# Weight conversions ahead of the first FFN: fourteen pieces in steps 1 to 94 instead of thirteen in steps 1 to 113

## The chip, the core and the metric

The kernel runs on one core of a Trainium2 chip. The metric is the device time of one execution in microseconds; the median of three executions stands for the kernel before. TensorE, VectorE (DVE), ScalarE (ACT), GpSimd (POOL) and SyncE (SP, which here only issues transfers) each work through an order of their own and wait for each other by semaphores. That order is fixed when the kernel is built.

## What is computed

The inputs are q, k and v of 8 batches, 12 heads, 448 tokens and 64 values a head, in float32, and two weight matrices of 768 x 3072 and 3072 x 768, stored as 64-bit floats.

```python
q_n, k_n = rmsnorm(q, g_q), rmsnorm(k, g_k)
attn = softmax(scale * q_n @ k_n.T) @ v        # per batch and head
x = attn                                       # as (batch, 448, 768)
u = x + real(fft(fft(x, axis=1), axis=2))
un = (u - mean(u)) / sqrt(var(u) + 1e-6)       # over the 768
out = u + maximum(un @ w_ch1, 0) @ w_ch2
```

## The kernel before

**Stages.** Each batch goes through attention, then the spectral part (the two Fourier transforms as matmuls, then the tiles `u` and `un`), then the FFN. `aux(b)` is a generator that yields after each small step of attention and spectral part of batch b; `ffn(b, unT)` is one that yields after each piece of weights. Attention works on six pairs of heads, each with softmax rows (`softmax_pair`), the norm and transposes of the next pair (`transpose_pair`) and the product with v (`value_pair`). `fold` prepares the Fourier transform along the 768 on VectorE. At the start, all 114 steps of `aux(0)` (0 to 113) run without an FFN beside them. Steps 0 to 94 are attention up to the point at which `attention(0)` fills the list `mixing`; in steps 95 to 113, which hold the last product with v, the last fold and the spectral part, each step is followed by one of the first fourteen steps of `aux(1)`. After that `merge` runs `ffn(0)` with the rest of `aux(1)`, `ffn(1)` with `aux(2)`, and so on.

**Weights.** The weights come as doubles. A piece is either 128 columns of w_ch1 (24 pieces, 128x768 values) or a 512x128 block of w_ch2 (36 pieces, 128x512 values): sixty in all. `convert` (from line 765) brings one piece in and splits it into a high and a low part for TensorE. It issues a DMA of the raw words into a tile `dbl` (L773, two buffers, tag X); ScalarE makes a float of the high words into a tile `mag` (L776, two buffers) and scales the low words in place (L777); VectorE clamps (L778), shifts (L782) and merges (L786); POOL adds the low part (L790); ScalarE rounds to the high part (L791); VectorE subtracts for the low part (L792). The result lies in one of three buffers of its stream and is also stored to DRAM (L820), from where later batches load it ready-made (L832).

**Two streams and early pieces.** Pieces are used in the order of the list `PIECES`; two streams of three buffers each hold them, in batch 0 by even and odd place. A stream's `load` takes its next piece: in batch 0 it converts it, unless the piece is in the set `early`; such a piece, and every piece of later batches, is loaded ready-made. The set is filled by `convert_some`, which is called after each step of `aux(0)` but the first, and which asks for a piece as soon as its account passes 1:

```python
conv = (p for n, p in enumerate(PIECES) if n % 8 in (3, 6))
def convert_some(share):
    debt[0] += share
    while debt[0] >= 1:
        p = next(conv)
        streams[stream_of(0, p)].converted(p, "e" + ...)
        early.add(p)
        debt[0] -= 1
```

In the trace the tiles of early pieces are named `dble`, `mage`, `w1e` and `w2e`; those of the pieces that the streams convert are `dbl`, `mag` and `w`. With 0.12 a step, pieces 1 to 13 are asked for after steps 9, 17, 25, 34, 42, 50, 59, 67, 75, 84, 92, 100 and 109. The twelfth and fourteenth in the list are 512x128 blocks of w_ch2, the thirteenth is a column piece of w_ch1. Once the 114 steps are through, each stream is asked for three pieces (`streams[n % 2].load()`, six in all), and then for another each time a piece has been used.

**What sets the order.** A scheduler of the framework orders each engine's instructions, in general by their place in the program, and lets a later instruction go first where an earlier one is not ready by its own estimate. The arithmetic of early pieces has one more rule: while `starting[0]` holds, `behind` puts each such instruction after the one that stands fourth from last among those already given to its engine by the other work. An early piece can therefore run only little ahead of the step after which it was asked for. Its DMA has no such rule. The main loop around the change (from line 1094):

```python
for n, _ in enumerate(aux(0)):
    if n == DFT_STEP:
        load_dft()
    if mixing:
        for _ in range(1):
            if next(ahead, None) is not None:
                next(second)
    if n:
        convert_some(CONVERT_EARLY)
starting[0] = False
```

Where all engines' operations go through one helper, the trace gives its line: L115 is the recorder of VectorE, ScalarE and POOL calls, so such instructions are told apart by their tiles. Other lines here: L644 is the first spectral matmul, L689 the write of `u` to DRAM, L888 the transposes of `un`, L1019 and L1040 the FFN's matmuls.

Of the kernel before, what the change touches and what calls it, by code (L numbers as in the profile page):

```python
# [38 lines left out]

RATIO = 0.49  # L40
RATIO_FIRST = 0.6
CONVERT_EARLY = 0.12
EARLY = 2
DFT_STEP = 40
AHEAD = 14
# [46 lines left out]
def spectral_block(ctx, tc, q, k, v, g_q, g_k, w1, w2, d1, d2, out, nb=B):  # L92
# [111 lines left out]
    def load_dft():  # L204
        nc.sync.dma_start(D1.rearrange("r i a n -> r (i a n)"), d1)
        st = slot("PT", "d2s")[:N1, : 4 * N1].rearrange("s (n t) -> s n t", n=4)
        for r in rows_of(N1):
            nc.sync.dma_start(st[r], d2[r].rearrange("s (n t) -> s n t", n=4))
        d2v = D2.rearrange("s i c a t -> s (i c) a t")
        A.copy(d2v[:, :, 0], st)  # L210
        sub(d2v[:, :, 1], st, d2v[:, :, 0])
# [321 lines left out]
    mixing = []  # L533
# [218 lines left out]
    def aux(b):  # L752

        EO, uns[b] = [], {}
        yield from attention(b, EO)
        yield from spectral(b, xTs[b], EO, uns[b])
# [117 lines left out]
# [5 lines that stand above are left out]
            streams[stream_of(0, p)].converted(p, "e" + "_".join(str(x) for x in p))  # L879
            early.add(p)  # L880
            debt[0] -= 1
# [215 lines left out]
# [4 lines that stand above are left out]
            for _ in range(1):  # L1101
                if next(ahead, None) is not None:
                    next(second)
        if n:
            convert_some(CONVERT_EARLY)
    starting[0] = False
    for n in range(6):
# [31 lines left out]
```

## Time and profile before

| what | value |
|---|---|
| median of three executions | 2156.36 us (2156.23 to 2157.32) |
| the profiled execution, its own time | 2157.21 us |
| its span in the trace | 2155.4 us |
| mean granted TensorE clock | 0.984 of full speed |
| DMA over the span | 423.88 MB, 197 GB/s |

The profile is that of one execution. Busy time of an engine is the time in which it ran an instruction of the program; TensorE's matmuls are pipelined and their ends are modelled, so a busy TensorE need not be one at its peak. The share of PEld (weight loads) says more of that. In the windows of the next section each row gives the stretch and its length, then for each engine the busy time and the number of instructions, the granted TensorE clock, the DMA engines' busy share, and GB/s. The chain of waits is followed back from the last instruction, at each step to what released it or to the instruction before it on its engine; its rows are start, length, and what it was.

### The profile page before, as it was taken

How to read it: one execution, taken by the hardware profiler on the slowest of the kernel's cores; microseconds unless marked ns; L12 is line 12 of the kernel's file. 1: busy time of each engine (PE TensorE's matmuls, PEld its weight loads, DVE VectorE, ACT ScalarE, POOL GpSimd, SP SyncE). 2: the span in 40 equal slices, each digit the busy share in tenths (PEclk: the TensorE clock that was granted, in tenths of full speed). 3: DMA queues.
4: the chain of work that ended last, by engine and by line, in shares of the span. 5: the costliest groups of instructions: out<-in, count | busy, mean ns of one | idle time of the engine just before them, and what ended most of it. 6: DMA issues, size and time to landing. Idle time of an engine off the chain costs nothing.

```text
span 2155.4 us, 31372 instructions
## 1 busy us (share of the span) xinstructions
PE 2079.3 (96%) x11256; PEld 1848.5 (86%) x11256; DVE 1544.9 (72%) x3002; ACT 1028.5 (48%) x2218; POOL 343.9 (16%) x200
## 2 busy tenths in 40 slices
PE   7877999999999999999999999999999999999998
PEld 4546777889999999999999999999999989999998
DVE  6787778887885788868787688857787578754122
ACT  6757876455552555335552455425553355422100
POOL 4324333321110111101110111101110011000000
PEclk8987999999999999999999999999999999999999
DMA  6547886687556855667566765558556674458874
GB/s 179 155 124 265 263 256 217 229 276 209 174 164 187 245 168 159 188 203 217 165 177 177 222 197 174 171 183 245 170 164 188 200 210 138 146 177 248 235 246 153
DMA packets 292913, 423.88 MB, mean 197 GB/s; under 512 B 181348, under 2 KB 219221, under 8 KB 292757
## 3 DMA queue, kind: packets, MB, share of 16 engines
q1 hardware_dynamic: 288322, 419.75, 64.1%
q10 hardware_dynamic: 4434, 2.11, 0.4%
q8 instruction: 90, 1.47, 0.3%
q14 instruction: 67, 0.54, 0.1%
HBM read 362.01 MB, written 65.31 MB: 198 GB/s over the span
## 4 chain that ended last, share of the span: by engine, by line
PE 79%; DVE 7%; DMA 6%; ACT 3%; issue 2%; POOL 2%; SPq 1%; POOLq 0%; DVEq 0%; ACTq 0%
PE o L1040 29%; PE h L1019 28%; PE S L407 5%; PE av L519 4%; PE pt L507 4%; DMA dbl<-w 3%; PE y L644 2%; POOL mag L790 1%; PE qk L343 1%; DVE mn L115 1%; DVE mag L786 1%; PE oT L976 1%; DMA u_dram<-u 1%; PE un L888 1%; DVE mag L778 1%
## 5 line engine op out<-in xcount | busy, mean ns | idle before, releaser
L1040 PE MATMUL o<-hs,w 128*128 128x448 f32 x3456 | 792.2, 372 | 4.9 <-DVE acc L115 3.2
L1019 PE MATMUL h<-unT,w 128*128 128x448 f32 x3456 | 783.0, 371 | 4.3 <-DVE hs L115 1.5
L1040 PEld LDWEIGHTS o<-hs,w 128*128 128x128 f32 x3456 | 637.7, 188 | 62.1 <-DVE acc L115 4.2
L1019 PEld LDWEIGHTS h<-unT,w 128*128 128x128 f32 x3456 | 640.0, 189 | 57.8 <-issue 2.2
L115 ACT ACTIVATE P<-S,mn 112x448 f32<-112x448 f32 x384 | 244.0, 638 | 222.5 <-DVE mn L115 208.7
L115 DVE TENSOR_REDUCE mn<-S 112x1 f32<-112x448 f32 x384 | 234.1, 617 | 43.3 <-PE S L407 34.1
L115 ACT ACTIVATE hs<-h 128x448 fp32r<-128x448 f32 x192 | 104.3, 543 | 277.9 <-PE h L1019 277.1
L115 DVE SCALAR_TENSOR_TENSOR hs<-h,hs 128x448 fp32r<-128x448 f32 x192 | 119.1, 620 | 129.8 <-ACT hs L115 128.4
L115 DVE TENSOR_TENSOR acc<-o,acc 128x448 f32<-128x448 f32 (+1 forms) x240 | 146.6, 613 | 87.9 <-PE o L1040 86.9
L115 POOL TENSOR_TENSOR qkn<-raw 112x1024 f32<-112x1024 f32 x36 | 69.4, 1927 | 686.4 <-PE qk L343 409.4
L115 POOL TENSOR_TENSOR ss<-ss,nhalf 112x16 f32<-112x16 f32 x48 | 142.0, 2959 | 203.8 <-DVE ss L115 195.1
L115 ACT CAST T<-pt 128x448 fp32r<-128x448 f32 x216 | 113.6, 533 | 124.7 <-PE pt L507 122.8
L115 DVE TENSOR_TENSOR T<-pt,T 128x448 fp32r<-128x448 f32 x216 | 132.3, 618 | 35.2 <-ACT T L115 34.1
L519 PE MATMUL av<-T,vhl 128*128 128x448 f32 x432 | 152.1, 384 | 0.0
L115 DVE TENSOR_SCALAR P<-P,sm 112x448 f32<-112x448 f32 x288 | 129.2, 487 | 4.6
L407 PE MATMUL S<-KD,QT 128*112 128x448 f32 x328 | 128.6, 392 | 2.2 <-ACT KD L115 1.9
L507 PE MATMUL pt<-ident,P 112*128 112x112 f32 x864 | 126.5, 258 | 0.0
L407 PE MATMUL S<-rounded,QT 128*112 128x448 f32 x328 | 120.4, 367 | 0.2 <-DVE rounded L115 0.2
L507 PEld LDWEIGHTS pt<-ident,P 112*128 112x128 f32 x864 | 104.3, 140 | 16.6
L790 POOL TENSOR_TENSOR mag<-mag,dbl 128x512 uint32<-128x512 uint32 (+1 forms) x47 | 78.8, 1677 | 159.3 <-DVE mag L786 131.2
L115 POOL TENSOR_TENSOR rstd<-st,nhalf 112x1 f32<-112x1 f32 (+2 forms) x32 | 19.6, 612 | 487.5 <-DVE st L115 480.5
L519 PEld LDWEIGHTS av<-T,vhl 128*128 128x128 f32 x432 | 80.9, 188 | 7.9
(120 smaller groups left out, 2499.5 us busy)
## 6 DMA issues: line engine op xcount, KB each, us to landing
w<-w SPq DMA_DIRECT2D x192, 768.0 KB, 4.5
w<-w SPq DMA_DIRECT2D x288, 512.0 KB, 3.9
dbl<-w SPq DMA_DIRECT2D x29, 512.0 KB, 4.8
dbl<-w SPq DMA_DIRECT2D x18, 768.0 KB, 4.9
raw<-q SPq DMA_DIRECT2D x96, 112.0 KB, 2.9
raw<-k SPq DMA_DIRECT2D x96, 112.0 KB, 5.0
values<-v SPq DMA_DIRECT2D x96, 96.0 KB, 4.4
u_dram<-u SPq DMA_DIRECT2D x24, 336.0 KB
```

Source lines behind the costliest of these rows:

```text
L115: ins = emit(*args, **kwargs)
L343: nc.tensor.transpose(pt[:, c * C : (c + 1) * C], qk[:, i, c].rearrange("t h d -> t (h d)"), ident[:C, :C],)
L407: ins = nc.tensor.matmul(s_, QT[:, h, cs], K[:, h], start=step == 0, stop=step == 1)
L507: nc.tensor.transpose(pt[:, c * C : (c + 1) * C], Pc[c][:, 512 * h + j * 128 : 512 * h + (j + 1) * 128], ident[:C, :C],)
L519: nc.tensor.matmul(av[:, :S], lv, T[:, i], start=(j == 0 and i == 0), stop=False)
L644: nc.tensor.matmul(o, src[:, par, t0 : t0 + n], D1[:, ri, par, cols], start=i != 1, stop=i != 0,)
L778: behind(nc.vector.tensor_scalar(out=value, in0=value, scalar1=MIN_HIGH, scalar2=MAX_HIGH, op0=ALU.max, op1=ALU.min,))
L786: behind(nc.vector.scalar_tensor_tensor(out=bits, in0=high, scalar=0xC0000000, in1=bits, op0=ALU.bitwise_and, op1=ALU.bitwise_or,))
L790: behind(nc.gpsimd.tensor_tensor(out=bits, in0=bits, in1=low, op=ALU.add))
L888: nc.tensor.transpose(pt[:, OFFS[i] : OFFS[i] + LENS[i]], uns[i][:, p * 128 : (p + 1) * 128], ident[: LENS[i], : LENS[i]],)
L1019: pace(nc.tensor.matmul(o, w[:, a, c], unT[c][:, z], start=n == 0, stop=n == 17))
L1040: pace(nc.tensor.matmul(o, w[:, a, f], hs[4 * g + f][:, z], start=n == 0, stop=n == 11))
```

## The change

The rate goes from 0.12 to 0.15 a step, and a step asks for conversions only while the list `mixing` is empty, which is so after steps 1 to 94. Pieces 1 to 14 are then asked for after steps 7, 14, 20, 27, 34, 40, 47, 54, 60, 67, 74, 80, 87 and 94. The fourteenth, a block of w_ch2 that has place 54 of 0 to 59 in the order of use, is no longer converted in the FFN of batch 0.

```diff
-CONVERT_EARLY = 0.12
+CONVERT_EARLY = 0.15
...
-        if n:
+        if n and not mixing:
             convert_some(CONVERT_EARLY)
```

## Rows read from the trace of the kernel before

**Rows 1.** The page, busy time of each engine, its share and instructions

```profile
PE 2079.3 (96%) x11256; PEld 1848.5 (86%) x11256; DVE 1544.9 (72%) x3002; ACT 1028.5 (48%) x2218; POOL 343.9 (16%) x200
```

**Rows 2.** Windows by stage: PE, PEld, DVE, ACT, POOL busy, clock, DMA share, GB/s

```profile
0.00:126.00 126.00, 98.58 (x457) 59.13 (x457) 94.52 (x159) 86.21 (x198) 46.27 (x35) 0.89 0.58 171
126.00:158.00 32.00, 23.15 (x126) 16.39 (x124) 25.67 (x48) 17.06 (x39) 6.64 (x3) 0.84 0.32 99
158.00:182.00 24.00, 8.33 (x40) 6.80 (x40) 20.44 (x45) 16.14 (x25) 10.52 (x7) 0.64 0.67 219
182.00:472.00 290.00, 274.32 (x1390) 231.88 (x1391) 234.93 (x407) 192.55 (x375) 102.79 (x64) 0.98 0.77 251
```

**Rows 3.** Windows, tile mage (early pieces): DVE, ACT, POOL busy; sum from 20 us

```profile
126.00:158.00 32.00, 2.20 (x4) 1.27 (x2) 1.44 (x1) 0.84 0.32 99
158.00:182.00 24.00, 3.35 (x4) 1.75 (x2) 1.83 (x1) 0.64 0.67 219
sum 162.00, DVE 34.88 ACT 19.70 POOL 20.89; mean DVE 4.98 ACT 2.81 POOL 2.98
```

**Rows 4.** Windows, tile mag (pieces converted by the streams): DVE, ACT, POOL busy

```profile
158.00:182.00 24.00, 10.04 (x11) 4.39 (x5) 6.03 (x3) 0.64 0.67 219
182.00:472.00 290.00, 119.00 (x177) 63.84 (x89) 72.81 (x44) 0.98 0.77 251
```

**Rows 5.** Chain of waits, 20 to 126 us: first and last of 31 conversion pieces

```profile
28.22 0.07 ACT w2e L791
...
122.84 0.84 ACT w2e L791
```

**Rows 6.** Chain of waits, 126 to 158 us: first and last of three conversion pieces

```profile
138.83 0.33 DVE mage L782
...
145.03 0.60 DVE w1e L792
```

**Rows 7.** Chain of waits, 157 to 183 us

```profile
160.29 0.47 DVE mage L778
...
161.63 0.54 DVE mag L778
...
163.64 2.01 DVE mag L782
...
170.21 0.74 ACT w L791
...
170.97 0.97 DVE w L792
171.94 0.92 ACT mag L776
...
172.89 0.56 DVE mag L778
...
173.95 6.57 DMA u_dram<-u
```

**Rows 8.** Timeline of the DMA queue on SP: start, length, issue

```profile
122.83 0.37 SPq L773 DMA_DIRECT2D dble<-w  x1
...
143.73 0.38 SPq L773 DMA_DIRECT2D dbl<-w  x1
```

**Rows 9.** Timeline, ScalarE: start, length, instruction

```profile
148.23 0.93 ACT L777 ACTIVATE dbl<-dbl 128x768 uint32<-128x768 uint32 x1 [3.88 <-DMA dbl<-w]
...
159.69 0.90 ACT L776 ACTIVATE mag<-dbl 128x768 f32<-128x768 f32 x1
```

**Rows 10.** Timeline, VectorE and POOL, 161 to 166 us

```profile
161.16 0.55 DVE L782 TENSOR_SCALAR mage<-mage 128x768 uint32<-128x768 uint32 x1
...
163.40 1.83 POOL L790 TENSOR_TENSOR mage<-mage,dble 128x768 uint32<-128x768 uint32 x1 [19.69 <-ACT un L115]
...
163.57 2.08 DVE L782 TENSOR_SCALAR mag<-mag 128x768 uint32<-128x768 uint32 x1
```

**Rows 11.** Windows, one full stretch of a later batch, columns as in rows 2

```profile
500.00:510.00 10.00, 10.00 (x60) 9.08 (x59) 9.03 (x20) 7.46 (x18) 1.89 (x1) 1.00 0.85 257
```

## The prediction

> **What bounds the kernel now.** I read the page first, then the stages by windows, then the conversions by their tiles in the same windows, then the chain of waits inside each stage.
>
> The page says that TensorE is busy for 96% of the span [rows 1]; the question is where the other 4% lies. The windows by stage answer it [rows 2]. I cut the span at 126 us (the last step before the mixing of the two batches is through; eleven early pieces are converted), at 158 us (the spectral part of batch 0 begins its last leg), at 182 us (the first FFN matmul) and at 472 us (FFN of batch 0 ends). I call the stages A, B, C, D, and E the rest. In A, B and C TensorE is busy 98.6 of 126, 23.2 of 32 and 8.3 of 24 us; in D 274.3 of 290. Beyond 472 us a typical stretch has TensorE busy 10.00 of 10 us with its weight loads at 9.08 [rows 11], so E has nothing to give. What the change can move lies in the first 472 us.
>
> In A, VectorE is busy 94.5 of 126 us (75%), in B 25.7 of 32 (80%), in C 20.4 of 24 (85%) [rows 2]. So up to 182 us the end is set by a chain that runs through VectorE and ScalarE, and conversions compete there. In D conversions share VectorE too, but TensorE is nearly full.
>
> The conversions are uneven. The early ones cost VectorE 34.88 us for thirteen, 2.68 us each; stage B holds only one (four VectorE instructions, 2.20 us) and C one (3.35 us) [rows 3]. C also holds eleven VectorE instructions, 10.04 us, of the pieces that the streams convert when the early ones are done: at four a piece 2.7 pieces, the other 44.3 being in D with 119.00 us [rows 4]. Of C's 20.4 us of VectorE, 13.4 are conversion.
>
> Why B is so empty shows in two places. Early piece 13 was asked for by the DMA queue at 122.83 us, and the next conversion load left only at 143.73 [rows 8]; there are two buffers for raw doubles, and the thirteenth piece sat in one of them until its arithmetic ran in C. The first stream piece had its low words scaled by ScalarE at 148.23 us, but its other ScalarE step came at 159.69 [rows 9], behind the thirteenth piece's. So the thirteenth, asked for at step 109, holds up all that follow it.
>
> **The change, part by part.** It does two things. The rate goes from 0.12 to 0.15 a step, and steps with mixing under way (95 to 113) ask for nothing. 113 steps by 0.12 made thirteen pieces, eleven of them by step 94; 94 by 0.15 is 14.1, so fourteen, all by step 94. Three more pieces therefore stand in stage A (two of 128x512 and one of 128x768), none is left over for B and C, and one piece fewer is converted in D, where it becomes a plain load. Each piece that moves takes its two DMA issues along on SP, its three ScalarE, four VectorE instructions and one POOL instruction. Sums are made against the profiled execution, 2157.21 us (span 2155.4 and 1.8 around it), which stands 0.85 above the median of the runs, 2156.36.
>
> Stage A, three pieces more. The lower end is 0: VectorE has 31.5 us idle there. The upper end by VectorE's work alone is 3 x 2.68 = 8.0. Between them lies the chain: in 20 to 126 us thirty-one bits of conversion stand on it, 19.6 us together [rows 5], which is 1.8 us for each of eleven pieces. Taking one away would not shorten the stage by all of that, since the chain would then run over another engine; I take 75% of it, VectorE's busy share, as it is VectorE that most of those bits hold: 3 x 1.8 x 0.75 = **+4.0**. The POOL adds stand ahead of the power of the next pair's sum of squares on POOL, and SP's six issues ahead of q, k and v loads; POOL is busy 46.3 of 126 us [rows 2], so I cost both at nothing beyond the 4.0. If that cover is gone, it is the norm of the next pair that is late.
>
> Stage B, piece 12 out, stream pieces in. Piece 12 put three bits on the chain just ahead of the first spectral matmul, 0.33, 0.60 and 0.60 us (first and last shown, three in all) [rows 6]: -1.5. VectorE's idle 6.3 us and the 2.2 freed hold three stream pieces at most (119.00 / 44.3 = 2.7 us each). I put two there. Their price is that of a conversion used as filler, which only D shows: TensorE is idle 15.7 us there, 0.35 us for each of 44.3 pieces, as the low end; the weight loads are busy 80% against 91% in a full stretch [rows 2, 11], which if it were all lost to conversions is 32 us or 0.72 each. I take 0.5 between the two: +1.0. B gives **-0.5**.
>
> Stage C, piece 13 out. Seven bits of conversion stand on its chain, 0.47, 0.54, 2.01, 0.74, 0.97, 0.92 and 0.56 us [rows 7]: 6.2 us for 3.7 pieces, 1.7 each. With two stream pieces through in B, two others slip into C (the six weight buffers and two raw buffers allow about five ahead of the FFN), so 3.7 become 2: **-2.9**. The ends are 0 (C as full as now) and -6.2 (empty). The 2.01 us is worth a look: an instruction that took 0.55 us on the same shape 2.4 us earlier took 2.08 while POOL's add ran from 163.40 [rows 10]. Such a stretch, 1.5 us, goes wherever the pieces go.
>
> Stage D. 46 pieces are left to the streams instead of 47, and four instead of 2.7 are done by its start: 42 against 44.3, 2.3 fewer at 0.5: **-1.1** (ends 0 and -1.7). The fourteenth piece's extra plain load is hidden like those of the other early pieces.
>
> Sum: 4.0 - 0.5 - 2.9 - 1.1 = -0.5, so 2156.7 against the profiled execution and 2155.9 against the median. The forecast is **no difference that can be told**; for this kernel that means within 0.2%, or 4.3 us.
>
> A rule speaks against the change. The Trainium skill's page "SBUF — State Buffer", section "SBUF: two separate sides", says that VectorE and GpSimd share one pair of ports, which whoever starts first holds for its whole instruction while the other waits, where VectorE has two SBUF inputs or uses both ports. The stretched instruction in rows 10 agrees. By the rule each of three more POOL adds in A can hold VectorE up once: at the 1.5 us of that row 4.5 us, and the sum would be +4.0 instead of -0.5. It is part of the second rival below, whose price is from rows alone.
>
> **The rivals.** *The freed buffers decide (faster).* If the streams, no longer behind piece 13, get five pieces through before 158 us, C is without conversions: A 4.0, B -1.5 + 5 x 0.5 = +1.0, C -6.2, and D has 41 pieces, 3.3 fewer at 0.5, -1.7. The write of u from 173.95 us, 6.57 us on C's chain [rows 7], would have fewer weight transfers beside it (C's DMA share is 0.67, B's 0.32 [rows 2]); I allow 2 us of it. Together -4.9, 2151.5 by the median; with A at its lower end it reaches 2147.5. For it: B's empty room and the 21 us gap between two loads. Against it: VectorE's room in B is three pieces, not five.
>
> *VectorE is the bound of A (slower).* Then each piece costs its whole VectorE time and the 1.5 us stretch by the POOL add: 3 x (2.68 + 1.5) = 12.5 in place of 4.0. The sum becomes +8.0, 2164.4 by the median. It decides from 2.9 us a piece on, where A's term passes 8.8 and the sum 4.3. For it: conversions asked for at a step stand in line with the attention's own work, not as filler, and the 1.8 us a piece that they already have on the chain. Against it: 25% of VectorE's time in A is idle, and a piece's VectorE work without the stretch is under 2.9.
>
> That fourteen are not reached is no rival: 14.1 leaves a margin.
>
> **How the numbers follow.** No difference 0.43, by the freed buffers 0.37, by VectorE in A 0.20. The orders on the engines are fixed when the kernel is built and will differ in many small places up to 472 us, which spreads each case by some 3 us. The likeliest case alone runs from 2152 to 2160. The range of 2147 to 2162 takes in the faster case down to A's lower end and the slower one up to somewhat past VectorE's 8.0 us without the stretch (-0.5 + 4.0 = +3.5); beyond it I leave about one in ten on either side. Chances: faster by over 0.2% 0.37, within 0.43, slower 0.20.
>
> **What would show it.** In the changed trace: fourteen early conversions, the last ending near 126 to 132 us; the first conversion load of the streams near 125 us instead of 143.73, with no gap of 21 us; in A some 8 us more VectorE work of conversions, and its end 4 us later; two or three stream pieces between there and the first spectral matmul; C, now 24 us, shorter by about 3; 42 pieces and about 1 us less TensorE idle in D; E unchanged. I am wrong if A grows by over 8 us, if the last leg loses over 6 us, or if the time beyond 472 us moves by more than 2 us.

## The result, and the profile after

The changed kernel is slower: 2169.61 us median of six executions (2167.05 to 2177.59) against 2156.84 us of the kernel before, a ratio of 1.0064 with a 95% interval of 1.005 to 1.0078. The forecast was no difference, in a range of 2147 to 2162 us; it was wrong. The profiled execution took 2167.05 us with a span of 2165.3, 9.9 us longer than that of before.

The page of the changed kernel, span and busy time of TensorE:

```profile
span 2165.3 us, 31385 instructions
...
PE 2077.6 (96%) x11256; PEld 1847.8 (85%) x11256; DVE 1557.3 (72%) x3002; ACT 1027.7 (47%) x2218; POOL 345.2 (16%) x200
```

TensorE does the same work (2079.3 us before [rows 1]); it waits longer. The windows of the changed kernel by stage, cut at its own first spectral matmul and first FFN matmul, columns as in [rows 2]:

```profile
0.00:126.00 126.00, 94.58 (x447) 56.79 (x447) 99.29 (x166) 90.51 (x203) 51.46 (x37) 0.91 0.64 189
126.00:155.00 29.00, 16.33 (x76) 9.58 (x74) 25.94 (x46) 17.48 (x36) 8.19 (x4) 0.78 0.57 175
155.00:190.00 35.00, 19.65 (x100) 17.03 (x100) 27.10 (x59) 20.14 (x35) 11.61 (x9) 0.60 0.72 240
190.00:484.00 294.00, 274.07 (x1395) 230.78 (x1395) 236.25 (x389) 184.23 (x362) 95.67 (x59) 0.98 0.70 229
```

The same windows for the tile mag alone, the pieces that the streams convert; the columns are VectorE, ScalarE and POOL. It answers to [rows 4]:

```profile
126.00:155.00 29.00, 5.06 (x8) 3.53 (x4) 1.84 (x1) 0.78 0.57 175
155.00:190.00 35.00, 14.07 (x18) 6.03 (x8) 9.97 (x6) 0.60 0.72 240
190.00:484.00 294.00, 114.94 (x158) 57.37 (x80) 64.41 (x39) 0.98 0.70 229
```

Before, no stream piece ran ahead of 158 us and eleven VectorE instructions of them after it. Now eight run ahead of the first spectral matmul and eighteen between it and the first FFN matmul, 6.5 pieces in all.

Two matmuls serve as landmarks of a run, the first spectral and the first FFN one. Timeline of TensorE in the kernel before:

```profile
147.53 2.05 PE L644 MATMUL y<-D,eo 128*113 128x130 f32 x8 [5.99 <-DVE eo L115]
...
182.01 0.74 PE L1019 MATMUL h<-unT,w 128*128 128x448 f32 x1 [1.36 <-ACT unT L115]
```

and of the changed kernel:

```profile
155.14 2.08 PE L644 MATMUL y<-D,eo 128*113 128x130 f32 x8 [2.75 <-DVE eo L115]
...
190.04 0.74 PE L1019 MATMUL h<-unT,w 128*128 128x448 f32 x1 [1.18 <-ACT unT L115]
```

So 7.6 us are lost up to the first spectral matmul, 0.4 between it and the first FFN matmul, 8.0 in all. The FFN of batch 0, which I count from there to the last transpose of un of batch 1 (471.7 us before, 483.9 after), takes 293.9 instead of 289.7 us, 4.2 more, and what follows takes 2.4 less: 8.0 + 4.2 - 2.4 = 9.8, the difference of the spans but for rounding.

Where the 7.6 us lie shows a third landmark, VectorE's write of `xT` for the fifth pair of heads, with which the fold of that pair can begin. Timeline of VectorE in the kernel before:

```profile
124.93 0.62 DVE L115 TENSOR_TENSOR xT<-rt,xT 128x448 f32<-128x448 f32 x1 [0.27 <-PE rt L450]
```

and in the changed kernel:

```profile
125.54 0.62 DVE L115 TENSOR_TENSOR xT<-rt,xT 128x448 f32<-128x448 f32 x1 [1.63 <-ACT xT L115]
```

From there to the first spectral matmul, which I call the fold stretch, it is 22.6 us before and 29.6 in the changed kernel: 0.6 of the 7.6 us are lost ahead of it and 7.0 in it. The window of this stretch before, columns as in [rows 2]:

```profile
124.90:147.50 22.60, 14.34 (x78) 8.73 (x75) 20.60 (x38) 13.35 (x31) 6.64 (x3) 0.85 0.45 138
```

and in the changed kernel:

```profile
125.50:155.10 29.60, 16.77 (x78) 10.02 (x78) 26.50 (x46) 17.92 (x38) 8.19 (x4) 0.78 0.57 176
```

VectorE is busy for 91% of the one and 90% of the other, and has eight instructions more in the changed kernel, those of the stream pieces, which take 5.06 us. At the first of them it also stands still: the piece's load has not landed, so ScalarE waits for the load and VectorE for ScalarE, with steps of the fold behind in the order (ScalarE, then VectorE):

```profile
129.31 0.90 ACT L776 ACTIVATE mag<-dbl 128x768 f32<-128x768 f32 x1 [1.62 <-DMA dbl<-w]
...
130.25 0.56 DVE L778 TENSOR_SCALAR mag<-mag 128x768 f32<-128x768 f32 x1 [1.79 <-ACT mag L776]
```

The 5.06 us of work and the 1.79 of waiting come near the 7.0. The later of the eight stand in VectorE's timeline of the changed kernel around the last fold (tiles eo, sd and tot; mag is a stream piece, mage the fourteenth early one):

```profile
145.82 1.15 DVE L115 TENSOR_TENSOR eo<-xT 128x449 f32<-128x449 f32 x2
146.89 0.68 DVE L792 TENSOR_TENSOR w1e<-mage,w1e 128x512 fp32r<-128x512 f32 x1
147.49 0.94 DVE L792 TENSOR_TENSOR w<-mag,w 128x768 fp32r<-128x768 f32 x1
...
151.37 1.03 DVE L778 TENSOR_SCALAR mag<-mag 128x768 f32<-128x768 f32 x2
152.31 1.29 DVE L115 TENSOR_TENSOR eo<-sd 128x226 f32<-128x226 f32 x4
153.52 1.02 DVE L782 TENSOR_SCALAR mag<-mag 128x768 uint32<-128x768 uint32 x2
154.46 0.62 DVE L115 SCALAR_TENSOR_TENSOR eo<-eo,eo 128x450 f32<-128x450 f32 x1
```

The spectral matmuls wait for that fold, and instructions of three stream pieces stand between its steps. After it, the chain of waits of the changed kernel runs through a load of a stream piece that ScalarE and VectorE then convert ahead of the spectral part's smdf:

```profile
163.06 7.04 DMA dbl<-w
...
170.18 0.67 ACT mag L776
...
171.92 1.60 DVE smdf L115 x2
```

ScalarE's order has that piece's step ahead of the copy bs of the spectral part. The waits of TensorE from 100 to 192 us show what this does:

```profile
PE ab L721 <- ACT bs L115: 6.4, 1, 6.4
```

TensorE stands 6.4 us for bs, against 0.8 before. What running stream pieces in this leg costs in all, the run with the hold tells below.

### The profile page after: what moved, and what is told of

Its sections match the earlier page's. It is cut to its first block, busy times and chain, and to the rows that moved or that the text cites. A ratio compares the mean times of both kernels' runs of the same rounds, so it can differ in the third digit from the quotient of the medians.

```text
span 2165.3 us, 31385 instructions
## 1 busy us (share of the span) xinstructions
PE 2077.6 (96%) x11256; PEld 1847.8 (85%) x11256; DVE 1557.3 (72%) x3002; ACT 1027.7 (47%) x2218; POOL 345.2 (16%) x200
## 4 chain that ended last, share of the span: by engine, by line
PE 79%; DMA 5%; DVE 5%; ACT 2%; issue 1%; POOL 1%; SPq 0%; DVEq 0%; POOLq 0%; ACTq 0%
PE o L1040 29%; PE h L1019 29%; PE S L407 6%; PE av L519 4%; PE pt L507 4%; DMA dbl<-w 3%; DMA u_dram<-u 2%; PE y L644 1%; PE qk L343 1%; PE oT L976 1%; POOL mag L790 1%; PE un L888 1%; DVE w L792 1%; PE av L524 1%; PE rem L462 1%
## 5 line engine op out<-in xcount | busy, mean ns | idle before, releaser
L115 DVE TENSOR_TENSOR T<-pt,T 128x448 fp32r<-128x448 f32 x216 | 132.5, 619 | 34.8 <-ACT T L115 33.5
L407 PE MATMUL S<-KD,QT 128*112 128x448 f32 x328 | 127.8, 390 | 4.6 <-ACT KD L115 3.1
```

The costliest lines, as they stand in the source:

```text
L115: ins = emit(*args, **kwargs)
L407: ins = nc.tensor.matmul(s_, QT[:, h, cs], K[:, h], start=step == 0, stop=step == 1)
```

## The experiments

**Theory 1** is that the loss ahead of the FFN comes from the place of the stream pieces. The **rival** is that the early pieces themselves, three more by step 94, cost the time. A table of the landmarks of all runs stands behind them; each line of it but the median is read from one execution. The kernel before ran again beside each group of runs, with medians of 2155.45 to 2156.84 us, and each ratio is to the one beside it. "Stream VectorE" counts VectorE instructions of stream pieces, ahead of the first spectral matmul and from there to the first FFN matmul.

**Fourteen pieces without the gate.**

```diff
-CONVERT_EARLY = 0.12
+CONVERT_EARLY = 0.125
```

> The kernel before with 0.125 a step in all steps: fourteen early pieces, spread over steps 8 to 112, no gate. Theory 1 (the loss comes from pieces of the streams that run before the spectral part, in which VectorE's order has none here against ten instructions in the changed kernel): the first spectral matmul at 146 to 150 us, the first FFN matmul at 184 or before, total within 4 us of before. Rival (the early pieces themselves cost, about 3 us for each one more): first spectral matmul 2 to 3 us later than before, total 3 us or more above before.

Measured: 2158.83 us, ratio 1.0011 (1.0001 to 1.002). The first spectral matmul came at 151.47 us, 1.5 beyond theory 1's end and 3.9 later than before, a little beyond the rival's 2 to 3; the first FFN matmul came at 184.62, and the total is 0.1% above before, 3.4 us by the medians. By these marks the run doesn't tell the two apart: theory 1 misses its times by 1.5 and 0.6 us, and the rival's 3 us or more is met. The trace does: the fold stretch is 22.1 us, as before, and all of the delay stands ahead of it, with xT at 129.4 us, though the run asks for eleven pieces by step 94, as the kernel before does. So a fourteenth early piece, without stream pieces in the folds, costs by the medians 3.4 us, and the change 12.8.

**Thirteen pieces with the gate.**

```diff
-CONVERT_EARLY = 0.12
+CONVERT_EARLY = 0.14
...
-        if n:
+        if n and not mixing:
```

> The changed kernel with 0.14 instead of 0.15: thirteen early pieces, all by step 94. Theory 1: VectorE's order again has ten instructions of stream pieces ahead of the first spectral result, so the first spectral matmul is at 153 to 157 us, the first FFN matmul at 187 to 192, total 6 to 13 us above before. Rival (the fourteenth piece, or the number of early pieces, is what costs): total within 4 us of before.

Measured: 2171.69 us, ratio 1.0074 (1.0059 to 1.0089), as slow as the changed kernel. Timeline of its TensorE, the same two matmuls:

```profile
157.13 2.05 PE L644 MATMUL y<-D,eo 128*113 128x130 f32 x8 [6.06 <-DVE eo L115]
...
192.37 0.74 PE L1019 MATMUL h<-unT,w 128*128 128x448 f32 x1 [1.90 <-ACT unT L115]
```

The number of early pieces is that of the kernel before; the loss is there all the same. The fourteenth piece is not what costs.

**The changed kernel with its stream pieces held.** The six first loads keep the rule of the early pieces, so that their arithmetic stands behind the fourth last instruction that the other work has given to each engine by then:

```diff
-    starting[0] = False
     for n in range(6):
         streams[n % 2].load()
+    starting[0] = False
```

> The changed kernel, with the arithmetic of the six first stream loads kept behind the other work of the first batch as that of early pieces is. Theory 1: first spectral matmul back at 147 to 150 us, first FFN matmul at 176 to 184; the FFN of batch 0 starts with fewer pieces ready and may give up to 6 us of it back; total within 5 us of before. Rival (fourteen pieces ahead of step 95 cost by themselves): first spectral matmul stays at 153 us or later, total 6 us or more above before.

Measured: 2144.68 us, ratio 0.9951 (0.9935 to 0.9968): the fastest of all runs, 25 us under the changed kernel's median and, by the ratio, 11 under the kernel before beside it. Timeline of its TensorE:

```profile
149.23 2.08 PE L644 MATMUL y<-D,eo 128*113 128x130 f32 x8 [1.40 <-DVE eo L115]
...
176.28 0.74 PE L1019 MATMUL h<-unT,w 128*128 128x448 f32 x1 [1.30 <-ACT unT L115]
```

and its window from the one to the other, tile mag alone:

```profile
149.00:176.00 27.00, 5.75 (x7) 2.60 (x3) 2.37 (x2) 0.69 0.28 85
```

Fourteen early pieces are as they were in the changed kernel; with the stream pieces away the first spectral matmul is 5.9 us earlier and the leg after it 7.9 us shorter. Theory 1 stands, the rival falls: fourteen pieces by step 94 leave the first spectral matmul 1.7 us later than before, no more. The fold stretch is 21.7 us, 0.9 shorter than before, and VectorE is busy for 97% of it:

```profile
127.50:149.20 21.70, 14.75 (x78) 9.36 (x78) 20.95 (x38) 12.36 (x30) 6.10 (x3) 0.89 0.53 166
```

The 1.7 us therefore stand ahead of the fold. ScalarE has two steps of the fourteenth piece ahead of its part of xT, and its load lands late:

```profile
125.87 0.66 ACT L776 ACTIVATE mage<-dble 128x512 f32<-128x512 f32 x1 [1.94 <-DMA dble<-w]
...
126.97 0.52 ACT L115 COPY xT<-av 128x448 f32<-128x448 f32 x1
```

The gain of the total is not all of this kind. Of the 23.0 us by which the span is shorter than the changed kernel's, 13.8 lie ahead of the first FFN matmul, 7.3 in the FFN of batch 0 and 1.9 behind that; of the 13.1 us against the kernel before it is 5.7, 3.2 and 4.3. The experiments explain only what lies ahead of the first FFN matmul.

**Two of the six loads free.**

```diff
-    starting[0] = False
     for n in range(6):
+        starting[0] = n >= 2
         streams[n % 2].load()
+    starting[0] = False
```

> The same, but the first two of the six stream loads are free and the last four are kept behind. VectorE's order has seven instructions of stream pieces ahead of the first spectral result instead of ten. Theory 1: between the changed kernel and the one above, first spectral matmul at 150 to 154 us. Rival: no different from the one above by more than 2 us.

Measured: 2155.93 us, ratio 0.9999 (0.9989 to 1.0009). Timeline of its TensorE:

```profile
155.41 2.08 PE L644 MATMUL y<-D,eo 128*113 128x130 f32 x8 [3.42 <-DVE eo L115]
...
182.27 0.74 PE L1019 MATMUL h<-unT,w 128*128 128x448 f32 x1 [1.25 <-ACT unT L115]
```

The first spectral matmul is as late as in the changed kernel, so two pieces free already cost the whole of it; the expected place between the two was missed. The leg after it is 26.9 us, as short as with all held. The two losses are separate: about 6 us in the folds, about 8 us after.

**The pieces free only after the last fold.** The six loads' arithmetic is put behind the last instruction given to each engine at step 103:

```diff
+        if n == 103:
+            folded.update({e: len(x) - 1 for e, x in given.items()})
     starting[0] = False
+    marks.update(folded)
     for n in range(6):
         streams[n % 2].load()
+    marks.clear()
```

(`behind` then orders such an instruction after `given[engine][marks[engine]]`.)

> The changed kernel, with the arithmetic of the six first stream loads kept behind the last fold alone (step 103), and free after it: no stream piece among the folds, but 23 VectorE instructions of them from the first spectral matmul on, as against 7 in the run that holds them to the end. If the two places add up (about 6 us lost ahead of the first spectral matmul, 8 us after it, as the run with two free loads has it): first spectral matmul at 147 to 151 us, first FFN matmul 33 to 36 us after it, total 2150 to 2157. If only the pieces among the folds cost: first FFN matmul 26 to 29 us after the first spectral one, total near 2145. If only those after it cost: as the changed kernel, 2165 or more.

Measured: 2160.31 us, ratio 1.0018 (1.0008 to 1.0027), a little above the range. Timeline of its TensorE (its lines are six further on):

```profile
149.47 2.08 PE L650 MATMUL y<-D,eo 128*113 128x130 f32 x8 [3.53 <-DVE eo L115]
...
183.36 0.74 PE L1025 MATMUL h<-unT,w 128*128 128x448 f32 x1
```

The first spectral matmul is where the hold has it, the leg after it 33.9 us. The two places add up as theory 1 says.

**The kernel before with the hold** (the same two lines moved).

> The kernel before (0.12, thirteen pieces in all steps) with the six first stream loads kept behind as in the run that was 11 us faster. It still has the thirteenth early piece in the last leg. If the hold alone makes that gain: total 2142 to 2148. If the early pieces must also be out of the last leg: first spectral matmul unchanged at 147 to 148 us, first FFN matmul 29 to 33 us after it, total 2150 to 2156.

Measured: 2153.83 us, ratio 0.9993 (0.9983 to 1.0002). First spectral matmul at 147.2, first FFN matmul 33.6 us after it, slightly beyond the 33 expected. The hold alone gains next to nothing; with fourteen early pieces it gains with the gate, which takes the early pieces out of the last leg. The gate's idea was right, then, if nothing fills the place.

**Fifteen, thirteen and twelve pieces with gate and hold** (0.16, 0.14 and 0.13 a step).

> The changed kernel with the stream loads held and 0.16 a step: fifteen early pieces by step 94 instead of fourteen. If early pieces cost nothing in the first 95 steps, as the traces so far have it: first spectral matmul at 147 to 151 us, total within 3 us of the run with fourteen, 2142 to 2148. If each one costs 3 us or so: 2147 or more, with the first spectral matmul 3 us later.

> The changed kernel with the six first stream loads held and 0.14 a step: thirteen early pieces by step 94. By the theory of place the first spectral matmul is at 146 to 151 us and the first FFN matmul 26 to 29 us after it. What follows is the test of the FFN of batch 0: the stretch from its first matmul to the last transpose of un of batch 1 was 286.5 us with fourteen pieces held and 300.9 with fifteen. If the number of pieces left to convert set it, thirteen would give 281 or 294 or something on a line with those; if it goes with the order alone, anything from 286 to 301, and the total from 2144 to 2160.

> As the run with fourteen pieces held, with 0.13 a step: twelve by step 94. With the runs of thirteen, fourteen and fifteen it gives what an early piece costs in the first 95 steps. If nothing: the transposes of the sums of the fifth pair at 123 to 126 us as with fourteen (124.9). If 1.3 us a piece, as the prediction had it: 122 to 123. If 2.9 (VectorE the bound): 119.

Measured: 2159.74 us (ratio 1.002, 1.0009 to 1.003), 2148.72 us (0.9973, 0.9964 to 0.9983) and 2145.79 us (0.996, 0.9946 to 0.9975). With twelve, thirteen, fourteen and fifteen pieces the transposes of the fifth pair's sums come at 123.3, 118.2, 124.9 and 127.8 us: no price per piece explains that order, though from twelve to fifteen it is 1.5 us a piece. (The eight executions that share the changed kernel's order up to there have it at 123.8 to 126.3.) Two expectations failed. The total with fifteen is not within 3 us of that with fourteen but 15 above it, with an FFN of batch 0 that is 14.4 us longer. The leg after the first spectral matmul is 34.2 us with thirteen and 35.3 with twelve, not 27. VectorE's timeline of the run with thirteen shows why:

```profile
158.50 1.54 DVE L115 TENSOR_TENSOR smdf<-ab,bs 112x390 f32<-112x390 f32 x2 [0.17 <-ACT bs L115]
...
164.11 2.09 DVE L782 TENSOR_SCALAR mag<-mag 128x768 uint32<-128x768 uint32 x1
166.24 0.96 DVE L786 SCALAR_TENSOR_TENSOR mag<-dbl,mag 128x768 uint32<-128x768 uint32 x1
...
167.17 0.55 DVE L115 SCALAR_TENSOR_TENSOR u<-x,smdf 112x384 f32<-112x384 f32 x1
```

and that of the run with fourteen held the same two steps without it:

```profile
164.94 1.56 DVE L115 TENSOR_TENSOR smdf<-ab,bs 112x390 f32<-112x390 f32 x2
167.73 0.56 DVE L115 SCALAR_TENSOR_TENSOR u<-x,smdf 112x384 f32<-112x384 f32 x1 [1.23 <-PE x L676]
```

From the start of smdf to that of u it is 8.7 us with six instructions of two stream pieces between them, and 2.8 without. Held by the same rule, the pieces got in there with thirteen and not with fourteen: again it is the place, not the number. What these two gain over the kernel before is therefore not the leg: with thirteen it is 3.7 us up to the first spectral matmul and 4.6 from the first FFN matmul on, with twelve 3.3 up to the first spectral matmul and 8.4 in the FFN of batch 0. And the FFN of batch 0 took 281.3, 288.6, 286.5 and 300.9 us with twelve to fifteen pieces, on no line.

**One load free.**

```diff
-    starting[0] = False
     for n in range(6):
+        starting[0] = n >= 1
         streams[n % 2].load()
+    starting[0] = False
```

> The changed kernel with the first of the six stream loads free and five held: VectorE's order has four instructions of stream pieces ahead of the first spectral result, against none with all held, seven with two free and ten with six free. If the loss ahead of the first spectral matmul grows with their number: it comes at 150 to 154 us, between 149.2 and 155.4. If two of them are enough to bring the ScalarE and POOL steps of a piece into the folds: 154 or later.

Measured: 2169.08 us, ratio 1.0066 (1.0047 to 1.0085). The first spectral matmul came at 155.82: one piece among the folds is enough. That the loss grows with their number is out. Its piece takes VectorE 3.0 us in four instructions, and the fold stretch is 28.5 us, 6.7 longer than with all six held. Most of the rest is again the wait for the load:

```profile
132.13 0.89 ACT L776 ACTIVATE mag<-dbl 128x768 f32<-128x768 f32 x1 [2.61 <-DMA dbl<-w]
...
133.05 0.56 DVE L778 TENSOR_SCALAR mag<-mag 128x768 f32<-128x768 f32 x1 [2.75 <-ACT mag L776]
```

The leg after it, 31.3 us, is 4.4 longer than with two free; why was not looked into.

**All stream pieces of batch 0 held** (the line `starting[0] = False` left out).

> The changed kernel with the arithmetic of all stream pieces of batch 0, not only of the first six loads, kept behind the fourth last instruction of the other work. Up to the first FFN matmul it should be as the run with six loads held: first spectral matmul 149, first FFN matmul 176 us. If pieces that run ahead of their place cost in the FFN of batch 0 as they do before it, that stretch falls below 286.5 us; if not, it stays within 3 us of 286.5 or grows.

Measured: 2163.84 us, ratio 1.0042 (1.0021 to 1.0063). First spectral matmul 150.2, first FFN matmul 177.5 us, as with six held. The FFN of batch 0 to the last transpose of un took 289.2 us, and what follows 22 us more than with six held. (The profiled execution, 2170.27 us, is the slowest of its five, 6.4 above their median.) A possible reason is that held pieces come too late for what uses them there: VectorE's last step of a stream piece ends at 483.6 us, against 449.4 with six held, and from 463 to 500 us TensorE is busy for 30.0 us, against 37.0. That would be 7 of the 22 us; no run tested it. Here the hold pays at the six first loads, and not when it is carried on.

**Three raw and three float buffers in the kernel before.**

```diff
-    SLOTS = {"P": 8, "PT": 6, "M": 2, "unT": 6, "h": 6}
+    SLOTS = {"P": 8, "PT": 6, "M": 3, "unT": 6, "h": 6}
...
-        return sb.tile([128, 1800], dtype, tag="X", name=name, bufs=2)
+        return sb.tile([128, 1800], dtype, tag="X", name=name, bufs=3)
```

> The kernel before with three buffers instead of two for the raw doubles and for the float pieces. The prediction said that the thirteenth piece, sitting in one of two raw buffers, held up the stream pieces. If that is so, stream pieces now run before the last leg and it is slower by 4 us or more. VectorE's order, though, still has no stream piece ahead of the first spectral result, so the theory of place expects the first spectral matmul at 146 to 149 us and a total within 4 us of before.

Measured: 2164.57 us, ratio 1.0039 (1.0024 to 1.0054). Its DMA queue and the first spectral matmul:

```profile
121.35 0.37 SPq L773 DMA_DIRECT2D dbl<-w  x1
...
150.09 2.08 PE L644 MATMUL y<-D,eo 128*113 128x130 f32 x8 [4.55 <-DVE eo L115]
```

The first stream load leaves at 121.35 us instead of 143.73 [rows 8], so the raw buffer did hold back the load. It alone did not hold back the arithmetic, of which none stands ahead of the first spectral matmul here either. The run is slower all the same: 4.1 us at the first FFN matmul and 4.4 us after the FFN of batch 0. Theory 1 had expected the first spectral matmul at 149 us at the latest and a total within 4 us of before; the total is 8.8 above. The fold stretch is 22.4 us, as before, so what is late at the first spectral matmul stands ahead of the fold, and theory 1 says nothing of that. Why the arithmetic stays away in the kernels without the gate, and comes in those with it, was not found.

**The FFN of batch 0 alone.** What was left were 4.2 us in that stage. Two runs of the changed kernel alter only how much of batch 1's attention goes beside it:

```diff
-RATIO_FIRST = 0.6
+RATIO_FIRST = 0.57
```

and 0.63.

> The changed kernel with 0.57 instead of 0.6 as the share of the second batch's attention beside the FFN of batch 0; VectorE's order up to the first FFN matmul is the same as in the changed kernel. If the 4 us more in the FFN of batch 0 (293.9 against 289.7) come with the change, as a stage entered with more pieces ready or later, they stay: 292 to 296 here as well. If they are one draw among many possible orders of that stage: it moves by 3 us or more, either way, with the first FFN matmul still at 189 to 191.

> The same with 0.63. If the 4 us come with the change: the stretch is again 292 to 296 us. If they are one draw among many orders: it moves by 3 us or more against the changed kernel or against the run with 0.57, with the first FFN matmul still at 189 to 191.

Measured: 2168.49 us (ratio 1.0052, 1.0033 to 1.0072) and 2156.28 us (1.0, 0.999 to 1.001). The first FFN matmul came at 190.3 and 191.9 us, the second 0.9 beyond the range, the stretch took 290.9 and 283.8 us against 293.9. With 0.63 it is 10 us shorter than in the changed kernel and 6 shorter than before, and the total is that of before although the FFN starts 10 us later. With 0.57 the stretch moved by 2.9 us, where the expectation asked for 3; with 0.63 it moved by 10. So the 4.2 us look like one draw among the orders of that stage: they don't stay when the pieces that are ready stay. What in an order makes it long or short was not found.

| run | early pieces | stream VectorE ahead / in the leg | fold stretch | first spectral | first FFN | leg | FFN of batch 0 | median |
|---|---|---|---|---|---|---|---|---|
| before | 13 | 0 / 11 | 22.6 | 147.5 | 182.0 | 34.5 | 289.7 | 2156.84 |
| changed | 14 | 8 / 18 | 29.6 | 155.1 | 190.0 | 34.9 | 293.9 | 2169.61 |
| 14, no gate | 14 | 0 / 4 | 22.1 | 151.5 | 184.6 | 33.2 | 289.7 | 2158.83 |
| 13, gate | 13 | 7 / 19 | 33.3 | 157.1 | 192.4 | 35.2 | 292.7 | 2171.69 |
| changed, hold | 14 | 0 / 7 | 21.7 | 149.2 | 176.3 | 27.0 | 286.5 | 2144.68 |
| two free | 14 | 6 / 9 | 28.3 | 155.4 | 182.3 | 26.9 | 294.0 | 2155.93 |
| one free | 14 | 4 / 11 | 28.5 | 155.8 | 187.1 | 31.3 | 296.1 | 2169.08 |
| free after the fold | 14 | 0 / 23 | 22.0 | 149.5 | 183.4 | 33.9 | 291.7 | 2160.31 |
| before, hold | 13 | 0 / 10 | 22.6 | 147.2 | 180.8 | 33.6 | 288.4 | 2153.83 |
| 15, gate, hold | 15 | 0 / 7 | 22.4 | 150.9 | 178.8 | 27.9 | 300.9 | 2159.74 |
| 13, gate, hold | 13 | 0 / 13 | 24.9 | 143.8 | 178.0 | 34.2 | 288.6 | 2148.72 |
| 12, gate, hold | 12 | 0 / 13 | 20.3 | 144.3 | 179.6 | 35.3 | 281.3 | 2145.79 |
| all held | 14 | 0 / 7 | 21.7 | 150.2 | 177.5 | 27.3 | 289.2 | 2163.84 |
| three buffers | 13 | 0 / 15 | 22.4 | 150.1 | 186.1 | 36.0 | 289.7 | 2164.57 |
| changed, 0.57 | 14 | 8 / 18 | 29.2 | 155.4 | 190.3 | 34.8 | 290.9 | 2168.49 |
| changed, 0.63 | 14 | 8 / 18 | 30.6 | 158.4 | 191.9 | 33.5 | 283.8 | 2156.28 |

All six runs with a stream piece ahead of the first spectral matmul have it at 155 us or later; all ten others at 151.5 or before. The fold stretch parts them more widely, at 28.3 to 33.3 us against 20.3 to 24.9. Much of the scatter of the first spectral matmul stands ahead of it: eight of these executions have one order on TensorE, VectorE, ScalarE and POOL up to the fifth pair's xT, and that comes between 125.5 and 128.4 us.

## Why the prediction was wrong

**Where the kernel is bound** was read rightly: nearly everything that moved in the changed kernel moved up to the end of batch 0's FFN. What follows it took 2.4 us less, a little more than the 2 us that I allowed.

**Stage A, three pieces more, +4.0.** Too high. VectorE is busy for 99.3 instead of 94.5 us there, yet the transposes of the fifth pair's sums come at 123.8 us against 124.2: -0.4. That is one pair of executions. Over the eight of the changed kernel's order they come at 124.8 on average, against 124.2 and 124.0 in the two of the order before: +0.7. The fifth pair's xT comes at 127.2 on average, against 124.9 and 124.6: +2.4; between the two landmarks lie the two ScalarE steps of the fourteenth piece and their wait. And only two of the three pieces are through by 126 us, with 52 VectorE instructions against 44; the fourteenth has four of its own in the fold. The second rival, VectorE as the bound of A, came nearer to the measured time with 2164.4, but by luck: A is not where the time went.

**Stage B, -0.5: the step that failed.** The forecast had the stream load leave near 125 us and two stream pieces run in B. The load left at 123.08:

```profile
120.29 0.37 SPq L773 DMA_DIRECT2D dble<-w  x1
...
123.08 0.37 SPq L773 DMA_DIRECT2D dbl<-w  x1
```

and eight instructions, two pieces' worth, ran there. Both terms of the -0.5 failed. The -1.5 for the twelfth piece did not come, because the fourteenth took its place: four VectorE instructions from 133.9 to 147.6 us, 2.19 us together, where the twelfth had four of 2.20 [rows 3], and not an end near 126 to 132 as I had it. And the +1.0 for the two stream pieces was mis-sized, and with it the sign of the stage. I took the 0.5 us a piece that a conversion seemed to cost in the FFN, where TensorE has other work at hand. Ahead of the first spectral matmul it has none: it waits for the folds, and the folds wait for VectorE. In the fold stretch the two pieces cost 7.0 us against the kernel before and 7.9 against the run with the hold, between 3.5 and 4 us each: 5.06 us of VectorE's time, and 1.79 in which VectorE stood for a load. The 1.7 us by which the first spectral matmul is late even with the hold stand ahead of the fold and are counted under A. "Filler" was my word for something that VectorE's order puts in fixed places.

**Stage C, -2.9.** The mechanism was right, and larger than I said: without early and free stream pieces the leg from the first spectral to the first FFN matmul falls from 34.5 to 27.0 us, 7.4 by the unrounded times, beyond my end of 6.2. But the pieces that the change frees take that place: I had two in C, it was eighteen instructions, four and a half pieces. The leg stayed at 34.9 us. (The chain there [rows 7] had two bits more, of 0.07 us each, than the seven that I counted.)

**Stage D, -1.1.** There the premise fell. 39.5 pieces were left instead of 44.3, and the stage took 4.2 us more. It ranged from 281 to 301 us over the runs, with no tie to the pieces left or ready; 0.35 to 0.72 us a piece was idle time divided by a number that no run shows to cause it.

**The first rival, freed buffers,** had the right event and the wrong sign. I listed VectorE's room in B against it, three pieces and not five, and did not draw the conclusion that what has no room is put in the way of the fold.

**The rule on the shared ports** (the Trainium skill's page "SBUF — State Buffer", section "SBUF: two separate sides") agrees with single instructions here too: a VectorE merge (line 786) took 1.93 us at 62.10 with POOL's add running from 61.83, against 0.96 for the same shape at 39.30, with nothing running on POOL. Not every POOL instruction held VectorE up: at 21.89 the same merge took 0.96 us while POOL's power of the sums of squares ran from 19.88 for 2.91 us, by a profile whose spans on POOL are rough. A came out below 4.0 all the same, so the 4.5 us more by that rule did not come.

## What to carry to other kernels

Work that is moved earlier frees what stood behind it; ask where that goes, and price it at the place where it lands, not at the place where it was cheap. Where a schedule fixes each engine's order, a piece of background work costs its own time and, if its load has not landed, the wait for that load, which all work behind it shares. So it can need a bound on how far ahead it may run as much as a deadline: here the change with such a bound was 0.5% faster than the kernel before, and without it 0.6% slower, though with one early piece more it was 0.2% slower even with the bound. A stage's idle time divided by the number of background pieces in it is no price: alter something else in the stage, and see whether it moves.

## What was not expected of the hardware

A load of 512 KB in the last leg took 7.04 us to land where the median of such loads was 5.3 in the same run, with the DMA engines busy for 72% of that stretch, and ScalarE stood 1.16 us for it, with the copy bs behind it in its order, whose input was ready at 165.5 us. Executions of one order are not alike either: the changed kernel and its two variants have the same order on VectorE up to the first FFN matmul, and the first spectral matmul came at 155.1, 155.4 and 158.4 us; most of that scatter, 125.5, 126.3 and 127.8 us, is there at the fifth pair's xT.
